# The first block's attention pair by pair of heads, in a written order, with products of zeros between

## Chip, core and metric

The kernel runs on one core of a Trainium2 chip. The metric is the device time of one execution in microseconds (us). The engines are TensorE (PE in the profile, PEld its weight loads), VectorE (DVE), ScalarE (ACT), GpSimd (POOL), and SyncE (SP), which here only issues the loads and stores.

## What is computed

Three layers over 2304 tokens (4 batches of 576) of width 512. The first is linear attention with a norm by head, the second a dense expert layer with a squared ReLU, the third a layer of eight routed experts:

```python
kv  = einsum('bhsd,bhse->bhde', k, v)          # 8 heads of 64
out = einsum('bhsd,bhde->bhse', q, kv)
out = out / sqrt(mean(out * out, -1) + 1e-6) * g_norm
x   = out.transpose(0, 2, 1, 3).reshape(2304, 512)
x   = relu(x @ w_in) ** 2 @ w_out              # 512 -> 2048 -> 512
# then: logits = x @ w_gate, one expert of 8 for each token, up to `capacity` tokens each,
# relu(x @ w1[e]) @ w2[e], times the gate's probability, back to the token's row
```

All inputs are 32-bit floats. The products of the dense layer are made of three passes of a rounded high part and a low part (`PASSES`: high·high, high·low, low·high), and so every operand of theirs has to be split into two tiles first.

## The kernel before

**Blocks and units.** Tokens are worked in six blocks of 384 (three tiles of 128). A unit (j, f) is block j with chunk f of the hidden width (16 chunks of 128): `mm1` makes 12 products of 128x384 into a PSUM bank `pk[s % 2]`, ACT and DVE square and split the result (L282 to L286), and two units later `mm2` adds 9 products of 128x512 into the block's three output banks. Units of block 0 come first, then blocks 0 and 1 by turns, then the others.

**Attention of a block.** `kv(b, p)` multiplies K and V of batch b and pair p of heads (5 products of fp32) and puts the two 64x64 blocks into the block-diagonal matrix `kvb` (ACT L212, DVE L213). `attn_out(t)` multiplies tile t of q with the four pairs into one bank, squares it on ACT (L236), sums by head on DVE (L238), and POOL makes the factor r as a power (L240, L242). `attn_mul` multiplies by r on DVE (L246), `attn_tr` transposes on PE (L255) and writes the high part (ACT, L259) and the low part (DVE, L260) of the operand `xT`. In block 0 this is done tile by tile, so the first output needs all four pairs.

**Weights of the dense layer.** A chunk f has an in-weight and an out-weight, each loaded as 64-bit words (`load_m`). `cvt_m` turns them into fp32: a first pass of ACT (L168, `ch`), then on DVE a first pass (L169) and a second pass (L170) over both weights, and a last pass for each (L174, `cf`). `split_m` rounds to the high part on ACT (L183) and makes the low part on POOL (L184).

**What sets the order.** SP's queue is in the order of the code: K and V of the four pairs of batch 0, then three tiles of q, then chunks 0 and 1 and what follows. The other engines' instructions are put in order by a scheduler's planner; each engine then runs its own list strictly in that order. At the start PE multiplies zeros nine times (`HOT`, L539). The line numbers in the profile are those of this file.

Of the kernel before, what the change touches and what calls it, by code (L numbers as in the profile page):

```python
# [7 lines left out]
F32 = mybir.dt.float32  # L8
F32R = mybir.dt.float32r
BF16 = mybir.dt.bfloat16  # L10
I32 = mybir.dt.int32
# [15 lines left out]
def attn_moe_kernel(ctx: ExitStack, tc: tile.TileContext, cap, kp, vp, qt, gn, wm, wg, wgt, w1, w2, ident, tri, out):  # L27
# [84 lines left out]
    def after_scatters(dma):  # L112
        dma = getattr(dma, "ins", dma)
        for i in scattered["disp"]:
            tc.add_manual_dep(
                dma, i.name, mybir.DependencyInfo(mybir.DependencyClass.Sync, mybir.DependencyReason.DATA),
                reason="reads what the scatters wrote",
            )


    kt, vt, qtt = {}, {}, {}
# [29 lines left out]
    def cvt_m(f):  # L151


        ws = [stg.pop(("m", f, i)).bitcast(I32).rearrange("p (n t) -> p n t", t=2) for i in range(2)]
        if f < 12:
            h = wpool2.tile([P, 2, 512], F32, tag="w", name="ch")
            o = wpool2.tile([P, 2, 512], F32, tag="w", name="cf")
            parts = [(h, o, slice(0, 2))]
            cvt[f] = [o[:, i, :] for i in range(2)]
        else:  # L160
            hs = [(apool1, apool)[i].tile([P, 1, 512], F32, tag="qx"[i], name="ch") for i in range(2)]
            os = [(apool, apool1)[i].tile([P, 1, 512], F32, tag="kv"[i], name="cf") for i in range(2)]
            parts = [(hs[i], os[i], slice(i, i + 1)) for i in range(2)]
            cvt[f] = [o[:, 0, :] for o in os]
        for h, o, sl in parts:
            hi, oi = h.bitcast(I32), o.bitcast(I32)
            for n, w in enumerate(ws[sl]):
                nc.scalar.activation(out=h[:, n, :], in_=w[:, :, 1].bitcast(F32), func=AF.Copy, scale=2.0 ** -112)  # L168
            nc.vector.tensor_scalar(oi, hi, -(1 << 31), None, op0=ALU.bitwise_and)  # L169
            nc.vector.scalar_tensor_tensor(  # L170
                out=oi, in0=hi, scalar=3, in1=oi, op0=ALU.logical_shift_left, op1=ALU.bitwise_or
            )
            for n, w in enumerate(ws[sl]):
                nc.vector.scalar_tensor_tensor(  # L174
                    out=oi[:, n, :], in0=w[:, :, 0], scalar=29, in1=oi[:, n, :],
                    op0=ALU.logical_shift_right, op1=ALU.bitwise_or,
                )

    def split_m(f, pool):
        os = cvt.pop(f)  # L180
        for o, d in zip(os, (wi, wo)):
            w = d[f] = pool.tile([P, 2, 512], F32R, tag="w", name="w")
            nc.scalar.copy(w[:, 0, :], o)  # L183
# [22 lines left out]
    def kv(b, p):  # L206
        k, v = kt.pop((b, p)), vt.pop((b, p))
        ps = misc()
        for c in range(NCH):
            nc.tensor.matmul(ps[:, :P], lhsT=k[:, c, :], rhs=v[:, c, :], start=c == 0, stop=c == NCH - 1)  # L210
# [52 lines left out]
        )  # L263


    gt = {}

    def mm1(s):
        j, f = units[s]
        h = pk[s % 2][:, :BT]  # L270
        n = 0
        for c in range(KD):
            for a, m in PASSES:
                nc.tensor.matmul(  # L274
                    h, lhsT=wi[f][:, a, c * P:(c + 1) * P], rhs=xT[j][:, m, c, :],
                    start=n == 0, stop=n == 3 * KD - 1,
                )
                n += 1


        r = gpool.tile([P, BT], F32, tag="rr", name="rr", bufs=2)
# [245 lines left out]
    MIDDLE = 416  # L527
    units = []

    with tc.manual_schedule(engines={mybir.EngineType.SP}):  # L530

        cold = gpool.tile([P, BT], F32, tag="rr", name="cold", bufs=2)[:, :P]
        nc.vector.memset(cold, 0.0)
# [1 line left out]
        for d in kvb:  # L535
            nc.vector.memset(d, 0.0)

        for i in range(HOT):
            nc.tensor.matmul(pk[0][:, :P], lhsT=cold, rhs=cold, start=True, stop=True)  # L539
# [16 lines left out]
        load_kv(1, 0)  # L556
# [5 lines left out]
        nc.sync.dma_start(out=tri_sb, in_=tri)  # L562
        for t in range(TB, 2 * TB):
            load_q(t)
        for p in range(NPAIR):
            kv(0, p)
        for t in range(TB):
            attn_out(t)
        for t in range(TB):
            attn_mul(t)  # L570
            attn_tr(t)
        for f in range(2):
            cvt_m(f)
            split_m(f, wpool)

        done_b = [1]

# [99 lines left out]
        for s in range(len(units)):  # L677
            j, f = units[s]
            if s == at[1, 0] + LAG:
                free.clear()  # L680
            mm1(s)
            if j == 0 and f + 3 < NF:
                load_m(f + 3)
            if j == 0 and f + 2 < NF:
                cvt_m(f + 2)
                split_m(f + 2, wpool if f + 2 < 12 else wpool2)
            if s >= LAG:
                mm2(s - LAG)
                jj, ff = units[s - LAG]
                if ff == NF - 1:  # L690
                    y_out(jj)
                    if jj < 2:
                        free[:] = ysets[jj]
            for p_ in plan.pop(s, []):
                p_()
            fl = s - at[NB - 1, 0]
# [379 lines left out]
```

## Time and profile before

| | us |
|---|---|
| median of 3 runs | 757.43 |
| lowest and highest | 756.63, 759.12 |
| the profiled execution | 755.1 |
| its span, first to last instruction | 753.2 |
| PE busy in the span | 715.7 |
| DVE busy | 371.6 |
| ACT busy | 309.5 |
| POOL busy | 292.3 |

A share of busy time is a mean over stages with different limits. The stage of this change is the first tenth of the span, where PE has waits; later it is full nearly all the time. In the rows "idle" in brackets is the time that the engine waited before the group, and the arrow names what ended it. An fp32 product of 128x128 leaves two records, and so five products of a pair stand as x10.

### The profile page before, as it was taken

Reading aid. Unit: us, or ns where it says so; the run is one execution under the profiler, and the core shown is the slowest. Engines: PE = TensorE matmul, PEld = TensorE weight load, DVE = VectorE, ACT = ScalarE, POOL = GpSimd, SP = SyncE. Lnnn points to the kernel's source line nnn. Section 1 sums busy time; section 2 is a strip of 40 time slices with the busy share of each in tenths; the row PEclk is TensorE's granted clock in tenths of the full one; section 3 lists DMA queues with packets and bytes.
Section 4 is the critical chain, followed back from the end, with each engine's and each line's share of the span. In section 5 each row is a group of like instructions: output and inputs, shape, how many; then the busy total and the mean of one; then the engine's idle time right before and its main releaser. Section 6 shows DMA issues by size and latency. Waiting matters only on the chain. (4 is left out here: it accounts for less than half of the span.)

```text
span 753.2 us, 12061 instructions
## 1 busy us (share of the span) xinstructions
PE 715.7 (95%) x4012; PEld 637.5 (85%) x4012; DVE 371.6 (49%) x833; ACT 309.5 (41%) x650; POOL 292.3 (39%) x288
## 2 busy tenths in 40 slices
PE   6678999999999999999999999999999999999985
PEld 6667999898899989989898988897888898889764
DVE  2989866548982594349634973331043221133011
ACT  2455454323222332233233264244276544376362
POOL 2566333112022200220130089043469746386881
PEclk9899999999999999999999999999999999999999
DMA  9946798401032202210010176043537554456530
GB/s 326 378 169 201 264 364 293 150 15 67 1 112 87 67 1 70 88 29 0 15 57 1 49 241 204 26 150 121 171 102 219 199 170 148 149 188 212 180 129 19
DMA packets 38016, 102.36 MB, mean 136 GB/s; under 512 B 4451, under 2 KB 4707, under 8 KB 37920
## 3 DMA queue, kind: packets, MB, share of 16 engines
q1 hardware_dynamic: 34912, 91.99, 36.4%
q0 software_dynamic: 3008, 9.10, 3.2%
q8 instruction: 59, 0.97, 0.5%
q14 instruction: 37, 0.30, 0.1%
HBM read 77.78 MB, written 23.91 MB: 135 GB/s over the span
## 5 line engine op out<-in xcount | busy, mean ns | idle before, releaser
L274 PE MATMUL pk<-xT,w 128*128 128x384 f32 x1152 | 223.1, 341 | 8.5 <-POOL w L184 4.6
L293 PE MATMUL pk<-w,g 128*128 128x512 f32 x864 | 218.4, 394 | 2.5 <-ACT g L285 2.5
L274 PEld LDWEIGHTS pk<-xT,w 128*128 128x128 f32 x1152 | 201.5, 188 | 18.6 <-POOL w L184 5.8
L195 POOL TENSOR_TENSOR w<-st,w 128x512 fp32r<-128x512 f32 x128 | 161.5, 1295 | 83.1 <-ACT w L191 83.0
L293 PEld LDWEIGHTS pk<-w,g 128*128 128x128 f32 x864 | 160.2, 188 | 31.7 <-ACT g L285 3.1
L282 ACT ACTIVATE rr<-pk 128x384 f32<-128x384 f32 x96 | 47.1, 492 | 153.6 <-PE pk L274 153.4
L817 PE MATMUL hb<-x,w 128*128 128x256 f32 (+2 forms) x672 | 96.7, 303 | 0.3
L817 PEld LDWEIGHTS hb<-x,w 128*128 128x128 f32 x672 | 93.8, 189 | 1.1 <-issue 0.2
L284 DVE TENSOR_TENSOR pk<-pk,rr 128x384 f32<-128x384 f32 x96 | 54.0, 563 | 74.6 <-ACT rr L282 73.7
L871 DVE SCALAR_TENSOR_TENSOR g<-hb,g 128x576 fp32r<-128x576 f32 (+3 forms) x72 | 40.5, 585 | 97.5 <-ACT g L870 96.5
L103 POOL DMA_INDIRECT disp<-y,sli x18 | 19.1, 1059 | 173.0 <-DVE sli L410 52.9
L355 DVE SCALAR_TENSOR_TENSOR junk<-y,wgb 128x512 f32<-128x512 f32 x120 | 78.0, 684 | 0.7 <-ACT y L313 0.6
L191 ACT CAST w<-st 128x512 fp32r<-128x512 f32 x128 | 71.7, 620 | 13.8 <-DMA st<-in_w 13.4
L285 ACT CAST g<-pk 128x384 fp32r<-128x384 f32 x96 | 46.0, 480 | 72.6 <-DVE pk L284 71.0
L286 DVE TENSOR_TENSOR g<-pk,g 128x384 fp32r<-128x384 f32 x96 | 53.3, 556 | 36.7 <-ACT g L285 36.0
L184 POOL TENSOR_TENSOR w<-cf,w 128x512 fp32r<-128x512 f32 x32 | 47.3, 1494 | 60.9 <-ACT w L183 56.3
L903 PE MATMUL hb<-w,g 128*128 128x512 f32 x264 | 65.7, 407 | 3.1 <-DVE g L871 2.5
L903 PEld LDWEIGHTS hb<-w,g 128*128 128x128 f32 x264 | 50.0, 193 | 15.7 <-DVE g L871 3.4
L870 ACT ACTIVATE g<-hb 128x576 fp32r (+3 forms) x72 | 34.9, 513 | 33.9 <-PE hb L817 29.2
L103 POOL DMA_INDIRECT out<-o,meta x22 | 21.3, 970 | 42.0 <-ACT o L911 17.8
L919 DVE SCALAR_TENSOR_TENSOR o<-bk,meta,o 64x512 f32<-64x512 f32 x3 | 2.3, 752 | 69.5 <-ACT o L918 51.0
L240 POOL TENSOR_SCALAR ms<-ss 128x8 f32<-128x8 f32 x18 | 4.6, 254 | 77.6 <-DVE ss L238 77.3
(138 smaller groups left out, 648.8 us busy)
## 6 DMA issues: line engine op xcount, KB each, us to landing
st<-in_w SPq DMA_DIRECT2D x64, 512.0 KB
st<-in_wm SPq DMA_DIRECT2D x32, 512.0 KB
disp<-zrow SPq DMA_DIRECT2D x9, 1028.0 KB
xr<-disp SPq DMA_DIRECT2D x32, 257.0 KB
k<-in_kp SPq DMA_DIRECT2D x16, 320.0 KB
v<-in_vp SPq DMA_DIRECT2D x16, 320.0 KB
q<-in_qt SPq DMA_DIRECT2D x18, 256.0 KB
out<-zrow SPq DMA_DIRECT2D x9, 512.0 KB
```

Source lines behind the costliest of these rows:

```text
L184: nc.gpsimd.tensor_tensor(w[:, 1, :], o, f32(w[:, 0, :]), op=ALU.subtract)
L191: nc.scalar.copy(w[:, 0, :], s[:, i, :])
L195: e.tensor_tensor(w[:, 1, :], s[:, i, :], f32(w[:, 0, :]), op=ALU.subtract)
L274: nc.tensor.matmul(h, lhsT=wi[f][:, a, c * P:(c + 1) * P], rhs=xT[j][:, m, c, :], start=n == 0, stop=n == 3 * KD - 1,)
L282: nc.scalar.activation(out=r, in_=h, func=AF.Relu)
L284: nc.vector.tensor_tensor(h, h, r, op=ALU.mult)
L285: nc.scalar.copy(g[:, 0, :], h)
L286: nc.vector.tensor_tensor(g[:, 1, :], h, f32(g[:, 0, :]), op=ALU.subtract)
L293: nc.tensor.matmul(ysets[j == 1][i], lhsT=g[:, a, i * P:(i + 1) * P], rhs=wo[f][:, m, :], start=f == 0 and n == 0, stop=f == NF - 1 and n ...
L355: nc.vector.scalar_tensor_tensor(out=junk, in0=yt[j * TB + i][:, :DM], scalar=1.0, in1=wgb[e // 2][:, e % 2, :], op0=ALU.mult, op1=ALU.mul ...
L817: nc.tensor.matmul(h, lhsT=w1_at(e, f // 2, a, c)[:, f % 2 * P:(f % 2 + 1) * P], rhs=x[:, m, c, o:o + w], start=k == 0, stop=k == 3 * KD - 1,)
L903: nc.tensor.matmul(ps[:k, :], lhsT=lhs(f, a), rhs=we2[e, f][:, b, :], start=n == 0, stop=n == len(passes) * NF2 - 1,)
```

## The change

Block 0's attention is written anew, pair by pair. The three tiles of q are loaded right after pair 0. For each pair p, `first_out` makes the three tiles' outputs of this pair (3 products into one bank) and squares them, `first_red` sums and makes the factor, `first_mul` multiplies, `first_tr` transposes and writes the high part, `first_low` the low part; operations on DVE and ACT are 384 wide instead of 512, four times instead of three. The transposes of a pair stand behind the outputs of the next. The pairs use six banks in turn instead of three.

The whole first part is taken out of the planner's hands: all engines run it in the order of the code. Three groups of products of zeros (`warm`, 4, 3 and 6) stand between. Chunk 0 is converted and split in two halves, the in-weight first, behind the low part of pair 2 and before the multiplication of pair 3. From there on the planner works as before, with two bounds on it that are no waits (`in_order`): the conversions of chunk 1 come after the last high part of the attention, those of the next chunk after chunk 1's last rounding, and the products of batch 1's pairs after the first unit's.

```diff
+    def in_order(later, first):
+        tc.add_manual_dep(
+            later, first.name, mybir.DependencyInfo(mybir.DependencyClass.NoSync, mybir.DependencyReason.SCHED_ONLY),
...
-            parts = [(h, o, slice(0, 2))]
+            parts = [(h[:, a:a + n], o[:, a:a + n], slice(a, a + n)) for a, n in (((0, 1), (1, 1)) if f == 0 else ((0, 2),))]
...
+            a = nc.scalar.activation(out=h[:, n, :], in_=w[:, :, 1].bitcast(F32), func=AF.Copy, scale=2.0 ** -112)
+            if "cvt" in marks:
+                in_order(a, marks["cvt"])
...
+    def split_m(f, pool, which=(0, 1)):
+        for i in which:
+            o = cvt[f][i]
...
+            a = nc.tensor.matmul(ps[:, :P], lhsT=k[:, c, :], rhs=v[:, c, :], start=c == 0, stop=c == NCH - 1)
+            if "kv" in marks:
+                in_order(a, marks["kv"])
...
+    def first_out(p):
+        ps = ops[p] = misc()
+        for t in range(TB):
+            nc.tensor.matmul(
+                ps[:, t * P:(t + 1) * P], lhsT=qtt[t][:, p, :], rhs=kvb[0][:, p, :],
+                start=t == 0, stop=t == TB - 1, skip_group_check=True,
+            )
...
+        nc.scalar.activation(out=x, in_=ps[:, :BT], func=AF.Square)
+
+    def first_red(p):
...
+        nc.vector.tensor_reduce(out=ss, in_=x.rearrange("p (h e) -> p h e", e=DH), axis=AX.X, op=ALU.add)
...
+        nc.gpsimd.tensor_tensor(r, ms, expo[:, :2 * TB], op=ALU.pow)
...
+    def first_tr(p):
+        x = xst.pop(p)
+        ps = misc()
+        for t in range(TB):
+            nc.tensor.transpose(ps[:, t * P:(t + 1) * P], x[:, t * P:(t + 1) * P], id_sb)
+        d = xt_tile(0)
+        marks["first"] = nc.scalar.activation(out=d[:, 0, p, :], in_=ps[:, :BT], func=AF.Copy, scale=gn_sb)
...
-    with tc.manual_schedule(engines={mybir.EngineType.SP}):
+    with tc.manual_schedule():
...
-        for p in range(NPAIR):
-            load_kv(0, p)
-            if p == 0:
-                nc.sync.dma_start(out=id_sb, in_=ident)
-                nc.sync.dma_start(out=gn_sb, in_=gn)
+        load_kv(0, 0)
+        nc.sync.dma_start(out=id_sb, in_=ident)
+        nc.sync.dma_start(out=gn_sb, in_=gn)
         for t in range(TB):
             load_q(t)
+        load_kv(0, 1)
+        load_kv(0, 2)
+        load_kv(0, 3)
...
+        free[:] = pk[2:8]
+        kv(0, 0)
+        first_out(0)
+        first_red(0)
+        warm(4)
+        kv(0, 1)
+        first_mul(0)
+        first_out(1)
+        first_red(1)
+        first_tr(0)
+        kv(0, 2)
+        first_low(0)
+        first_out(2)
+        first_mul(1)
+        first_red(2)
+        kv(0, 3)
+        first_out(3)
+        first_red(3)
+        first_tr(1)
+        first_low(1)
+        warm(3)
+        first_mul(2)
+        first_tr(2)
+        first_low(2)
+        c_in, c_out = cvt_m(0)
+        c_in()
+        split_m(0, wpool, (0,))
+        warm(6)
+        first_mul(3)
+        first_tr(3)
+        first_low(3)
+        c_out()
+        split_m(0, wpool, (1,))
...
+    with tc.manual_schedule(engines={mybir.EngineType.SP}):
+        marks["cvt"] = marks["first"]
+        for c in cvt_m(1):
+            c()
+        split_m(1, wpool)
+        marks["cvt"] = marks["split"]
```

PE's list from the pairs of batch 0 to the second unit, before (`v,k` are a pair's products, `kvb,q` the outputs, `id_sb,x` the transposes, `xT,w` the units of the dense layer, and `pk_88`, `pk_89` their banks):

```order
L210 MATMUL pk_93<-v,k 128x128 x5
L228 MATMUL pk_94<-kvb_128,q 128x128 x4
L228 MATMUL pk_95<-kvb_128,q 128x128 x4
L228 MATMUL pk_93<-kvb_128,q 128x128 x4
L255 MATMUL pk_94<-id_sb,x 128x128 x4
L255 MATMUL pk_95<-id_sb,x 128x128 x4
L255 MATMUL pk_93<-id_sb,x 128x128 x4
L210 MATMUL pk_94<-v,k 128x128 x5
L210 MATMUL pk_95<-v,k 128x128 x5
L210 MATMUL pk_93<-v,k 128x128 x5
L210 MATMUL pk_94<-v,k 128x128 x3
L274 MATMUL pk_88<-xT,w 128x384 x2
```

All pairs come first there, then all outputs, then all transposes. The end of the same stretch now (`cold` are the zeros):

```order
L224 MATMUL pk_91<-v,k 128x128 x5
L286 MATMUL pk_92<-kvb_128,q 128x128 x3
L314 MATMUL pk_93<-id_sb,x 128x128 x3
L602 MATMUL pk_88<-cold 128x128 x3
L314 MATMUL pk_94<-id_sb,x 128x128 x3
L602 MATMUL pk_88<-cold 128x128 x6
L314 MATMUL pk_95<-id_sb,x 128x128 x3
L334 MATMUL pk_88<-xT,w 128x384 x12
L224 MATMUL pk_93<-v,k 128x128 x5
L224 MATMUL pk_94<-v,k 128x128 x5
L224 MATMUL pk_95<-v,k 128x128 x5
L334 MATMUL pk_89<-xT,w 128x384 x12
```

The products of batch 1's pairs, which stood ahead of the first unit, now stand behind it.

DVE's list at the end of the attention, before (`st_176` and `st_178` are chunk 0's two weights, `st_180` and `st_182` chunk 1's; `kvb_129` is batch 1's matrix):

```order
L246 TENSOR_TENSOR x<-pk_95,r 128x512
L169 TENSOR_SCALAR cf<-ch 128x1024
L260 SCALAR_TENSOR_TENSOR xT<-pk_94,gn_sb,xT 128x4x128
L260 SCALAR_TENSOR_TENSOR xT<-pk_95,gn_sb,xT 128x4x128
L246 TENSOR_TENSOR x<-pk_93,r 128x512
L170 SCALAR_TENSOR_TENSOR cf<-ch,cf 128x1024
L169 TENSOR_SCALAR cf<-ch 128x1024
L260 SCALAR_TENSOR_TENSOR xT<-pk_93,gn_sb,xT 128x4x128
L174 SCALAR_TENSOR_TENSOR cf<-st_176,cf 128x512
L174 SCALAR_TENSOR_TENSOR cf<-st_178,cf 128x512
L170 SCALAR_TENSOR_TENSOR cf<-ch,cf 128x1024
```

The conversions stand between the attention's steps there. DVE's list at the same place now:

```order
L321 SCALAR_TENSOR_TENSOR xT<-pk_94,gn_sb,xT 128x384
L183 TENSOR_SCALAR cf<-ch 128x512
L184 SCALAR_TENSOR_TENSOR cf<-ch,cf 128x512
L188 SCALAR_TENSOR_TENSOR cf<-st_176,cf 128x512
L305 TENSOR_TENSOR x<-pk_92,r 128x384
L321 SCALAR_TENSOR_TENSOR xT<-pk_95,gn_sb,xT 128x384
L183 TENSOR_SCALAR cf<-ch 128x512
L184 SCALAR_TENSOR_TENSOR cf<-ch,cf 128x512
L183 TENSOR_SCALAR cf<-ch 128x1024
L188 SCALAR_TENSOR_TENSOR cf<-st_178,cf 128x512
L184 SCALAR_TENSOR_TENSOR cf<-ch,cf 128x1024
```

The first passes of chunks 0 and 1 and chunk 0's second pass, which stood between the attention's steps, now come one weight at a time, chunk 0's in-weight before the last multiplication and everything else after the last low part.

## Rows read from the trace of the kernel before

**Rows 1.** The page, part 1: busy us (share of the span) and instructions, TensorE

```profile
PE 715.7 (95%) x4012; PEld 637.5 (85%) x4012; DVE 371.6 (49%) x833; ACT 309.5 (41%) x650; POOL 292.3 (39%) x288
```

**Rows 2.** Table by stretches: from:to, length, busy of each engine, granted clock, DMA share, GB/s

```profile
5.00:10.00 5.00, 3.19 (x23) 2.86 (x22) 0.77 (x5) 0.41 (x2) 0.00 (x0) 1.00 0.98 330
10.00:15.00 5.00, 4.76 (x40) 4.52 (x41) 0.95 (x3) 1.24 (x4) 0.00 (x0) 1.00 1.05 414
15.00:20.00 5.00, 1.26 (x10) 0.85 (x8) 2.88 (x6) 2.75 (x5) 4.38 (x6) 0.94 1.03 400
20.00:25.00 5.00, 2.63 (x12) 2.29 (x13) 4.27 (x6) 2.20 (x4) 2.14 (x4) 0.50 1.03 402
...
30.00:35.00 5.00, 2.93 (x16) 2.41 (x14) 4.89 (x4) 1.70 (x4) 5.00 (x4) 1.00 1.04 414
...
75.00:80.00 5.00, 5.00 (x27) 4.47 (x26) 4.44 (x7) 2.64 (x6) 2.12 (x2) 1.00 0.94 315
```

**Rows 3.** Timeline of TensorE: start us, busy us, engine, line, operation, tiles, count, [idle before]

```profile
7.70 1.35 PE L210 MATMUL pk<-v,k 128*128 128x128 f32 x10 [1.02 <-DMA v<-in_vp]
...
11.44 1.35 PE L210 MATMUL pk<-v,k 128*128 128x128 f32 x10 [0.24 <-DMA v<-in_vp]
...
18.11 0.63 PE L255 MATMUL pk<-id_sb,x 128*128 128x128 f32 x4 [2.49 <-DVE x L246]
20.12 1.08 PE L255 MATMUL pk<-id_sb,x 128*128 128x128 f32 x4 [1.38 <-DVE x L246]
...
24.34 5.30 PE L210 MATMUL pk<-v,k 128*128 128x128 f32 x36
...
31.16 2.39 PE L274 MATMUL pk<-xT,w 128*128 128x384 f32 x12 [0.63 <-POOL w L184]
35.08 2.03 PE L274 MATMUL pk<-xT,w 128*128 128x384 f32 x10 [1.52 <-POOL w L184]
...
37.16 1.06 PE L228 MATMUL pk<-kvb,q 128*128 128x128 f32 x8
```

**Rows 4.** Table by stretches, the 27.7 us in which DVE is nearly full

```profile
26.10:53.80 27.70, 22.88 (x139) 19.72 (x138) 24.65 (x32) 15.79 (x33) 18.27 (x13) 1.00 0.74 268
```

**Rows 5.** Timeline of all engines: steps of the attention, first roundings and low parts

```profile
9.33 0.23 DVE L213 COPY kvb<-pk 64x64 f32<-64x64 f32 x1 [1.80 <-ACT kvb L212]
...
14.50 0.69 DVE L238 TENSOR_REDUCE ss<-x 128x8 f32<-128x512 f32 x1 [1.21 <-ACT x L236]
...
17.28 0.69 DVE L246 TENSOR_TENSOR x<-pk,r 128x512 f32<-128x512 f32 x1 [1.19 <-POOL r L242]
...
25.30 0.75 DVE L260 SCALAR_TENSOR_TENSOR xT<-pk,gn_sb,xT 128x512 fp32r<-128x512 f32 x1 [0.26 <-ACT xT L259]
...
29.03 2.18 ACT L183 CAST w<-cf 128x512 fp32r<-128x512 f32 x4
...
29.73 9.91 POOL L184 TENSOR_TENSOR w<-cf,w 128x512 fp32r<-128x512 f32 x6 [7.51 <-ACT w L183]
```

**Rows 6.** DVE by line and shape, 0 to 27 us: count, busy us, mean ns, idle

```profile
L169 DVE TENSOR_SCALAR cf<-ch 128x1024 int32<-128x1024 int32 x2 | 1.4, 682 | 0.0
L174 DVE SCALAR_TENSOR_TENSOR cf<-st,cf 128x512 int32<-128x512 int32 x2 | 1.3, 682 | 0.0
L170 DVE SCALAR_TENSOR_TENSOR cf<-ch,cf 128x1024 int32<-128x1024 int32 x1 | 1.2, 1212 | 0.0
```

**Rows 7.** Timeline of DVE: a second pass beside POOL, and the last row considered

```profile
31.70 2.20 DVE L170 SCALAR_TENSOR_TENSOR cf<-ch,cf 128x1024 int32<-128x1024 int32 x1
...
53.83 0.69 DVE L246 TENSOR_TENSOR x<-pk,r 128x512 f32<-128x512 f32 x1 [0.94 <-POOL r L242]
```

**Rows 8.** DVE by line and shape, 26.1 to 53.8 us: the conversions

```profile
L174 DVE SCALAR_TENSOR_TENSOR cf<-st,cf 128x512 int32<-128x512 int32 x10 | 8.9, 933 | 0.1
L170 DVE SCALAR_TENSOR_TENSOR cf<-ch,cf 128x1024 int32<-128x1024 int32 x4 | 6.3, 1584 | 0.0
L169 DVE TENSOR_SCALAR cf<-ch 128x1024 int32<-128x1024 int32 x3 | 2.8, 920 | 0.0
```

More of the change, by code (lines that the diff above doesn't have):

```diff
@@ L118, in after_scatters @@
             )
+    def in_order(later, first):
+        later, first = getattr(later, "ins", later), getattr(first, "ins", first)
+        tc.add_manual_dep(
+            later, first.name, mybir.DependencyInfo(mybir.DependencyClass.NoSync, mybir.DependencyReason.SCHED_ONLY),
+            reason="the order in which the loads come in",
+        )
+    marks = {}
     kt, vt, qtt = {}, {}, {}
@@ L164, in cvt_m, with cvt_part @@
             cvt[f] = [o[:, 0, :] for o in os]
[L165 to L169, printed above, removed]
+        return [lambda part=part: cvt_part(ws, *part) for part in parts]
+    def cvt_part(ws, h, o, sl):
+        hi, oi = h.bitcast(I32), o.bitcast(I32)
+        for n, w in enumerate(ws[sl]):
+            a = nc.scalar.activation(out=h[:, n, :], in_=w[:, :, 1].bitcast(F32), func=AF.Copy, scale=2.0 ** -112)
+            if "cvt" in marks:
+                in_order(a, marks["cvt"])
+        nc.vector.tensor_scalar(oi, hi, -(1 << 31), None, op0=ALU.bitwise_and)
+        nc.vector.scalar_tensor_tensor(
+            out=oi, in0=hi, scalar=3, in1=oi, op0=ALU.logical_shift_left, op1=ALU.bitwise_or
+        )
+        for n, w in enumerate(ws[sl]):
             nc.vector.scalar_tensor_tensor(
-                out=oi, in0=hi, scalar=3, in1=oi, op0=ALU.logical_shift_left, op1=ALU.bitwise_or
-            )
[L173 to L183, printed above, removed]
+                out=oi[:, n, :], in0=w[:, :, 0], scalar=29, in1=oi[:, n, :],
+                op0=ALU.logical_shift_right, op1=ALU.bitwise_or,
+            )
+    def split_m(f, pool, which=(0, 1)):
+        for i in which:
+            o = cvt[f][i]
+            w = (wi, wo)[i][f] = pool.tile([P, 2, 512], F32R, tag="w", name="w")
+            marks["split"] = nc.scalar.copy(w[:, 0, :], o)
             nc.gpsimd.tensor_tensor(w[:, 1, :], o, f32(w[:, 0, :]), op=ALU.subtract)
@@ L263, in attn_tr, with first_mul, first_low @@
         )
+    def first_out(p):
[4 more added lines that the diff above has]
+                start=t == 0, stop=t == TB - 1, skip_group_check=True,
+            )
+        x = xst[p] = ypool.tile([P, ROW], F32, tag="y", name="x")[:, :BT] if p < 3 else apool.tile(
+            [P, DM], F32, tag="x", name="x")[:, :BT]
+        nc.scalar.activation(out=x, in_=ps[:, :BT], func=AF.Square)
+    def first_red(p):
+        x = xst[p]
+        ss = small.tile([P, 2 * TB], F32, tag="ss", name="ss")
+        nc.vector.tensor_reduce(out=ss, in_=x.rearrange("p (h e) -> p h e", e=DH), axis=AX.X, op=ALU.add)
+        ms = small.tile([P, 2 * TB], F32, tag="ms", name="ms")
+        nc.gpsimd.tensor_scalar(ms, ss, 1.0 / DH, 1e-6, op0=ALU.mult, op1=ALU.add)
+        r = rst[p] = small.tile([P, 2 * TB], F32, tag="r", name="r")
+        nc.gpsimd.tensor_tensor(r, ms, expo[:, :2 * TB], op=ALU.pow)
+    def first_mul(p):
+        r, ps = rst.pop(p), ops.pop(p)
+        nc.vector.tensor_tensor(
+            xst[p].rearrange("p (h e) -> p h e", e=DH), ps[:, :BT].rearrange("p (h e) -> p h e", e=DH),
+            r.rearrange("p (h o) -> p h o", o=1).to_broadcast([P, 2 * TB, DH]), op=ALU.mult,
+        )
+    def first_tr(p):
[5 more added lines that the diff above has]
+        marks["first"] = nc.scalar.activation(out=d[:, 0, p, :], in_=ps[:, :BT], func=AF.Copy, scale=gn_sb)
+        ops[p] = ps
+    def first_low(p):
+        d, ps = xt_tile(0), ops.pop(p)
+        nc.vector.scalar_tensor_tensor(
+            out=d[:, 1, p, :], in0=ps[:, :BT], scalar=gn_sb, in1=f32(d[:, 0, p, :]), op0=ALU.mult, op1=ALU.subtract,
+        )
     gt = {}
@@ L536, in attn_moe_kernel, with warm @@
             nc.vector.memset(d, 0.0)
-        for i in range(HOT):
-            nc.tensor.matmul(pk[0][:, :P], lhsT=cold, rhs=cold, start=True, stop=True)
+        def warm(n):
+            for _ in range(n):
+                nc.tensor.matmul(pk[0][:, :P], lhsT=cold, rhs=cold, start=True, stop=True)
+        warm(HOT)
         nc.gpsimd.iota(tok, pattern=[[P, NT]], base=0, channel_multiplier=1)
@@ L564, in attn_moe_kernel @@
             load_q(t)
-        for p in range(NPAIR):
-            kv(0, p)
-        for t in range(TB):
[L568 to L574, printed above, removed]
+        free[:] = pk[2:8]
[31 more added lines that the diff above has]
+        split_m(0, wpool, (1,))
+        for t in range(TB):
+            qtt.pop(t)
+        free[:] = ysets[1]
+    with tc.manual_schedule(engines={mybir.EngineType.SP}):
[4 more added lines that the diff above has]
+        marks["cvt"] = marks["split"]
         done_b = [1]
@@ L684, in attn_moe_kernel @@
             if j == 0 and f + 2 < NF:
-                cvt_m(f + 2)
+                for c in cvt_m(f + 2):
+                    c()
+                marks.pop("cvt", None)
                 split_m(f + 2, wpool if f + 2 < 12 else wpool2)
```

7 lines of the change are left out of this document (5 added, 2 removed).

## Prediction

> **What bounds the kernel now.** I read the page's busy times first: TensorE (PE) is busy 95% of the span [rows 1], so a change in the first stage is worth only the PE time that it takes out of the start. The table by stretches comes next: PE is full from 75 us on [rows 2], and until then it has holes. The timeline of PE shows what they are: waits for loads up to 11.4 us, then for the transposes' input, then for weights: the first expert product runs at 31.16, the second chunk's at 35.08, and everything up to the first tile of block 1 is done at 37.16 + 1.06 = 38.2 us [rows 3]. The last look is at VectorE (DVE) between 26.1 and 53.8 us. It is busy 24.65 of 27.70 us there [rows 4], and what PE waits for at that time (weights, hidden values, tiles of block 1) has gone through it. So two things bound the start: first the serial chain of the attention, then DVE's queue. A gain in the first counts only as far as DVE's queue also ends sooner.
>
> **The loads.** SP's queue now asks for the three q tiles right behind pair 0 and before pairs 1 to 3. The bytes in front of the weights are the same, so no weight lands earlier or later. Before, pair 1 came in by 7.70 and pair 3 by 11.44 us [rows 3]. 0.79 MB of q now stand where 0.66 MB of pair 1 stood: at the rates of [rows 2] (330 GB/s in 5 to 10 us, 414 in 10 to 15) q is there at about 8.05, pair 1 at 10.2, pair 2 at 11.8 and pair 3 at 13.3 us.
>
> **The chain of the attention.** Five fp32 products, two records each, take 1.35 us [rows 3], so three take 0.8. From the end of a pair's products to its block on the diagonal I take 0.5 us (ACT copy, then the DVE copy of 0.23), from the start of the reduction to the multiplication 17.28 - 14.50 = 2.78, at three quarters of the width 2.6, and for a DVE step of 0.69 to 0.75 us some 0.55 [rows 5]; ScalarE's steps alike. Walked: pair 0's outputs start with q, 8.1 to 8.9 (before, no output could start until pair 3's products had ended at 11.44 + 1.35 = 12.8 [rows 3]); square and the 2.6 us put its multiplication at 12.0 and its end at 12.6. Pair 1's products run 10.2 to 11.55, its outputs, 0.5 later, to 12.9, and behind them on PE the transposes of pair 0 to 13.4; pair 2 to 14.75, outputs 15.25 to 16.1; pair 3 to 17.45, outputs 17.95 to 18.8; transposes of pair 1 at 19.3. Pair 2's square, 2.6 us and multiplication lead from 16.1 to 21.1, so its transposes end at 21.7. Then DVE, whose order is now written out, converts the first half of chunk 0 (0.35 + 0.62 + 0.62, half of [rows 6]) before it multiplies pair 3: that ends at 25.2, its transposes at 25.8, its low part at 26.9. Before, the last low part ended at 25.30 + 0.75 = 26.05 [rows 5]. So the attention of the first block, though it starts 4 us earlier, ends 0.85 us later: 17 us of single file with DVE waiting in each step.
>
> **The zeros and the clock.** 13 products of zeros at 0.27 us stand where PE waits anyway: 8.9 to 9.95 (pair 1 comes at 10.2), 19.3 to 20.1 (next needed 21.2), 21.7 to 23.3 (25.2). They cost nothing; if pair 1 landed sooner, at most 0.3. What they may keep is the clock: before, PE did 1.26 us of work in 15 to 20 us, then the granted clock fell to 0.50 [rows 2] and four transposes took 1.08 instead of 0.63 us [rows 3]. In the walk above PE works 2.3 us of 20 to 25, between that 1.26 and the 2.93 that held at 30 to 35 [rows 2]. If it falls, ten of the first expert products (0.2 us each [rows 3]) double, up to 2.0 us, but ScalarE takes them up only at 30.2 (it rounds the second half of chunk 0 first), so the sum has 0 for it and 0.4 as the far end. POOL's two short tasks for later buffers stand between the factors of pairs 2 and 3, and one waits for the transposes of pair 1; pair 3's factors are there at 22, needed at 24.7, so this is hidden, with 2.7 us to spare.
>
> **The first expert products.** Chunk 0's first weight is rounded at 24.7 and its low part made by 26.7, against 29.03 [rows 5] and 31.1, for which the row of 31.16 waited [rows 3]: the first unit ends at 28.9 instead of 33.2 (ten more products from 31.16 on [rows 3]). That is 4.3 us. But products of batch 1's pairs, which filled PE's waits before (36 half passes in 5.30 us [rows 3]), now stand behind it: three pairs, 4.05 us, to 33.0. The second unit needs chunk 1, whose conversion DVE now begins at 28.3 (before, its first pass and chunk 0's were both done by 27 us [rows 6]): its low part comes at about 34.1, and it ends at 36.2 against 37.1. The fourth pair (1.35) and the first tile of block 1 (1.06) then end at 38.6, against 38.2. The 4.3 us are used up: the same work is done at the same time, in another order.
>
> **DVE's queue.** From 26.1 us to the multiplication at 53.83 [rows 7], DVE spent 27.70 us: 3.05 idle, and 24.65 busy [rows 4]. Of the busy time, the conversions lost (933-682) ns x 10 + (1584-1212) x 4 + (920-682) x 3 = 4.7 us against their prices before 27 us [rows 6, 8]: POOL's low parts run beside them here, not there. So 19.95 us are work. In the changed order the same multiplication has more ahead of it, from 26.9 on: the first and second pass of half of chunk 0 (0.34 + 0.62) and chunk 1's first pass (0.60), but one last pass less (0.60), so about 1.0 us more. 26.9 + 19.95 + 1.0 = 47.85, plus what is lost. With the same 7.75 us lost it is 55.6, 1.8 us behind. I estimate less: chunk 0's first low part (25.3) meets only operations that read PSUM; the others meet part of chunk 1's second pass (0.4), chunk 2's first (0.6), chunk 3's first and second (1.7), chunk 4's (1.2): 3.9 to 4.0. Idle: 1.1 where DVE waits at about 33.9 for ScalarE's first pass of chunk 2 (its queue has two roundings and two copies first), 0.5 for a tile's factors (0.94 in the last row [rows 7]), and some 0.6 of short gaps: 2.2. So 47.85 + 4.0 + 2.2 = 54.05, +0.2 us. From there on both programs have the same instructions in the same order, so this difference stays to the end. Bounds: losses of 3 to 9.5 us, -3 to +3.5.
>
> A rule to weigh here: the row of 31.70 shows a second pass at 2.20 us beside POOL where 1.21 is its price alone [rows 6, 7], so I let both run on at half pace. [...]
>
> **The rivals.** *The gain carries.* POOL's low parts all fall beside PSUM reads, so 1.5 us of stretch and 1.3 of waits remain: 47.85 + 2.8 = 50.65, 3.2 us ahead, 754.2. For it: the lows start 4.4 us earlier and come two at a time, not six in a row [rows 5]. Against: every chunk still has two lows and 3.2 us of passes, and DVE has no slack to step aside. *DVE stays behind.* The place is 27 to 45 us: DVE enters 0.85 us late with 1.0 us more to do; if the lost time is not smaller than before (7.75) and ScalarE's late first pass of chunk 2 (1.1) comes on top, +2.9 us: 760.3. It counts as slower from losses of 8.3 us on (2.3 us behind). For it: the written order lets nothing overtake in the first 27 us. Against: the run of six lows on end is gone. *The clock falls early.* If the pauses of 12 to 26 us already take it, 5.5 us of products on the chain double and everything follows: 762.9. The zeros and 3.9 us of work in 15 to 20 speak against it. That the change would not do what it says can be left out: the order shows it.
>
> **How the numbers follow.** The profiled execution took 755.1 us (span 753.2, 1.9 around it); the median of the runs is 757.43, 2.3 more. The sum, +0.2, makes 755.3 for such an execution and 757.6 for the median. Chances: forecast 0.76, the gain carries 0.12, DVE stays behind 0.10, the clock 0.02. A measurement of this kernel can tell about 0.3%, 2.3 us, from no change, so faster 0.12, same 0.76, slower 0.12. The range takes in no change on both sides, and half of the slower rival: 755.0 to 760.2; most of the first rival and the last are left out.
>
> **What would show it.** Right: first unit's products end near 29 us, the low part of pair 3 ends near 27, the second unit ends within 1 us of 37, PE is full from 75 to 76 us, and DVE's conversions between 27 and 54 us lose 3 to 5 us. Wrong: PE full by 73 us (DVE lost under 3.7 us in all), or only from 78 on; a granted clock of 0.50 before 22 us; a low part of pair 3 later than 28.5.

## The result: slower by 4.6 us, and where it shows

| | before | after |
|---|---|---|
| median of 16 runs each | 756.72 us | 761.76 us |
| lowest and highest | 755.03, 759.96 | 758.18, 766.66 |
| the profiled execution (its span) | 755.1 (753.2) | 758.18 (756.4) |

The ratio is 1.0061, with a 95% interval of 1.0046 to 1.0077; in a second set of runs (7 of after) it is 1.0070 (1.0044 to 1.0097). The forecast was no change, 757.6 us, with 755.0 to 760.2 as its range: it is wrong, and by a mechanism that none of its cases held.

The page, part 1, after, for [rows 1]; 26 more records of PE are the 13 products of zeros, two for each:

```profile
PE 718.8 (95%) x4038; PEld 640.2 (85%) x4038; DVE 370.4 (49%) x838; ACT 310.2 (41%) x652; POOL 291.1 (38%) x290
```

The table by stretches of after, for [rows 2] and [rows 4] (columns as there):

```profile
5.00:10.00 5.00, 4.15 (x26) 3.56 (x24) 0.41 (x2) 0.70 (x2) 0.00 (x0) 1.00 0.99 354
...
15.00:20.00 5.00, 3.98 (x31) 3.60 (x31) 2.75 (x7) 1.66 (x4) 3.44 (x6) 1.00 1.02 391
20.00:25.00 5.00, 1.89 (x15) 1.70 (x15) 3.67 (x7) 1.35 (x3) 1.52 (x2) 1.00 1.03 407
...
26.84:30.25 3.41, 3.41 (x11) 3.41 (x12) 3.37 (x6) 2.00 (x4) 0.00 (x0) 0.50 1.04 356
...
27.20:53.40 26.20, 22.86 (x140) 20.34 (x140) 23.75 (x35) 16.23 (x34) 15.30 (x12) 0.94 0.75 266
```

The timeline of PE in after, for [rows 3]: first outputs, first and second unit, first tile of block 1, and the last wait before PE is full:

```profile
7.59 1.67 PE L286 MATMUL pk<-kvb,q 128*128 128x128 f32 x6 [0.62 <-DVE kvb L229]
...
26.83 3.56 PE L334 MATMUL pk<-xT,w 128*128 128x384 f32 x10 [0.58 <-POOL w L198]
...
34.43 2.03 PE L334 MATMUL pk<-xT,w 128*128 128x384 f32 x10 [0.34 <-POOL w L198]
...
37.41 1.06 PE L244 MATMUL pk<-kvb,q 128*128 128x128 f32 x8
...
70.85 2.63 PE L355 MATMUL pk<-w,g 128*128 128x512 f32 x6 [2.48 <-ACT g L347]
73.28 2.87 PE L334 MATMUL pk<-xT,w 128*128 128x384 f32 x12
...
76.69 2.28 PE L334 MATMUL pk<-xT,w 128*128 128x384 f32 x12
```

DVE in after, for [rows 5, 7]: the low part of pair 3, and the multiplication to which the prediction's sum was made:

```profile
26.55 0.62 DVE L321 SCALAR_TENSOR_TENSOR xT<-pk,gn_sb,xT 128x384 fp32r<-128x384 f32 x1 [1.31 <-ACT xT L316]
...
53.35 0.67 DVE L262 TENSOR_TENSOR x<-pk,r 128x512 f32<-128x512 f32 x1
```

So the first stage went as walked: the low part of pair 3 ends at 27.2 us (forecast 26.9), the second unit at 36.5 (36.2), the first tile of block 1 at 38.5 (38.6), and the multiplication is at 53.35 (54.05), half a microsecond ahead of before instead of 0.2 behind. PE is then full from 76.69 us on, against 75.58 in the profiled execution of before; but that is the granted clock, which fell to 0.50 behind the wait at 70.85 here and not in that execution. In another execution of before it fell there too, and PE is full from 77.17 on:

```profile
71.58 2.93 PE L293 MATMUL pk<-w,g 128*128 128x512 f32 x6 [2.45 <-ACT g L285]
...
77.17 2.28 PE L274 MATMUL pk<-xT,w 128*128 128x384 f32 x12
```

Like for like the start is 0.5 us ahead. The loss lies behind 500 us, in the routed experts, which the diff does not touch. Their code has branches: by an expert's count of tokens each engine jumps over the products that it doesn't need. Four places in TensorE's list are used below: **A**, the transposes behind the first expert's branches, near 517 us; and in the last expert **B**, two transposes near 725, **C**, its first products `hb<-w,x` near 735, and **D**, its third group `bk<-w,x` near 740. The timeline of PE there, before:

```profile
517.34 1.08 PE L796 MATMUL bk<-id_sb,xr 128*128 128x128 f32 x8 [1.34 <-issue]
...
723.21 0.30 PE L859 MATMUL hb<-id_sb,turned 128*128 128x128 f32 x1 [0.29 <-issue]
...
725.73 7.34 PE L903 MATMUL hb<-w,g 128*128 128x512 f32 x24 [0.99 <-DVE g L871]
...
733.25 1.66 PE L842 MATMUL hb<-w,x 128*128 128x256 f32 x12
...
738.05 1.69 PE L842 MATMUL bk<-w,x 128*128 128x256 f32 x12
```

And after, the same instructions in the same order:

```profile
519.84 1.08 PE L899 MATMUL bk<-id_sb,xr 128*128 128x128 f32 x8 [2.48 <-issue]
...
726.86 0.41 PE L962 MATMUL hb<-id_sb,turned 128*128 128x128 f32 x2 [1.35 <-ACT gl L979]
...
734.71 1.68 PE L945 MATMUL hb<-w,x 128*128 128x256 f32 x12 [0.51 <-issue]
...
741.20 1.67 PE L945 MATMUL bk<-w,x 128*128 128x256 f32 x12 [1.51 <-ACT gl L979]
```

A waits 1.1 us longer, B 1.1, C 0.5, D 1.5. "issue" says that nothing in the profile released A and C. `gl`, named at B and D, is only the last thing that ACT had done; what these need is a copy `turned` (the operand of B's transposes, and the bank that D writes), and the timeline of ACT in after has both copies done 1.2 and 1.3 us before B and D start:

```profile
725.32 0.37 ACT L964 COPY turned<-bk 128x256 f32<-128x256 f32 x1 [0.66 <-PE bk L945]
...
739.50 0.37 ACT L964 COPY turned<-bk 128x256 f32<-128x256 f32 x1 [0.22 <-PE bk L945]
```

Over the whole stretch from full speed to the last product, PE's idle time in the records is 13.2 us before and 16.7 after. With 1.1 us at the start, and 1.5 that before lost in 726.0 to 729.4 us at half clock (24 products in 7.34 us, 5.82 at full clock) and after did not, that is 1.1 + 3.5 - 1.5 = 3.1 of the 3.2 us between the two spans.

### The profile page after: what moved, and what is told of

It reads as the page before. It is cut to its first block, busy times and chain, and to the rows that moved or that the text cites. A ratio compares the mean times of both kernels' runs of the same rounds, so it can differ in the third digit from the quotient of the medians.

```text
span 756.4 us, 12119 instructions
## 1 busy us (share of the span) xinstructions
PE 718.8 (95%) x4038; PEld 640.2 (85%) x4038; DVE 370.4 (49%) x838; ACT 310.2 (41%) x652; POOL 291.1 (38%) x290
## 5 line engine op out<-in xcount | busy, mean ns | idle before, releaser
L334 PE MATMUL pk<-xT,w 128*128 128x384 f32 x1152 | 225.9, 343 | 6.3 <-POOL w L198 3.3
L346 DVE TENSOR_TENSOR pk<-pk,rr 128x384 f32<-128x384 f32 x96 | 54.0, 563 | 75.4 <-ACT rr L344 74.5
L205 ACT CAST w<-st 128x512 fp32r<-128x512 f32 x128 | 71.6, 620 | 13.4 <-DMA st<-in_w 12.9
L198 POOL TENSOR_TENSOR w<-cf,w 128x512 fp32r<-128x512 f32 x32 | 44.6, 1409 | 64.2 <-ACT w L197 59.6
L1006 PE MATMUL hb<-w,g 128*128 128x512 f32 x264 | 64.1, 399 | 2.1 <-DVE g L974 1.8
L973 ACT ACTIVATE g<-hb 128x576 fp32r (+3 forms) x72 | 34.9, 512 | 33.9 <-PE hb L920 26.1
```

The costliest lines, as they stand in the source:

```text
L205: nc.scalar.copy(w[:, 0, :], s[:, i, :])
L334: a = nc.tensor.matmul(h, lhsT=wi[f][:, a, c * P:(c + 1) * P], rhs=xT[j][:, m, c, :], start=n == 0, stop=n == 3 * KD - 1,)
L1006: nc.tensor.matmul(ps[:k, :], lhsT=lhs(f, a), rhs=we2[e, f][:, b, :], start=n == 0, stop=n == len(passes) * NF2 - 1,)
```

## Experiments

Three theories stood against each other: the clock (zeros at the start, a lower clock later), the written order of the first stage, and, once the waits at A to D had been seen, the place of TensorE's code: how many of its instructions stand ahead. One 32-bit product is four of them (two weight loads, two products, as the records show), so the 13 zeros are 52; the changed kernel's code stands 51 further back, since it has one wait fewer (407 records of waits and branches on TensorE, 408 before).

**Both kernels again, the zeros away, more zeros.** The zeros: `warm` 4, 3, 6 to none; and 3 to 8, 6 to 15.

```diff
-        warm(4)
...
-        warm(3)
+        warm(8)
...
-        warm(6)
+        warm(15)
```

> The kernel before once more, for a second trace and the granted clock of each of its executions. Clock theory (the 4.6 us are TensorE's clock, granted low in more stretches of the changed kernel): mean granted clock about 0.991 in most executions, and times that rise where it is lower. Queue theory (the written order makes a later start of the full stretch at full clock): no difference of clock between the kernels; this one 757 us with TensorE full from 75.6 us.

> The changed kernel once more. Clock theory: 761 to 763 us, mean granted clock 0.985 to 0.989, and in the trace at least two more stretches at 0.5 than in the first trace, which had two ahead of the tail (26.8 and 71.2 us) and was the quickest of its 16 executions. Queue theory: the same stretches at 0.5 as in the first trace, and TensorE full only 3 to 4 us later than before's 75.6 us with the clock full.

> The changed kernel without its 13 products of zeros behind the start (output unchanged; the nine at the very start stay). Clock theory: the clock falls earlier or for longer before 30 us, and the time is 1 to 3 us longer than the changed kernel's. Queue theory, and my prediction's sum: they stand in waits, so no change (within 1 us).

> The changed kernel with 8 and 15 products of zeros instead of 3 and 6 ahead of the transposes of pairs 2 and 3, which fills the waits of 1.28 and 2.37 us there. Clock theory: the first units run at full clock (the first one's last ten products 2.0 instead of 3.6 us), mean granted clock up by 0.004 or more, 1.5 to 4 us less than the changed kernel. Queue theory: first unit 1.5 us sooner, but the end no more than 0.5 us sooner, since DVE's queue is not.

Measured: before again 756.4 us (ratio 0.9999, 0.998 to 1.0019), after again 760.21, no zeros 759.74 (1.0040, 1.0024 to 1.0056), more zeros 763.34 (1.0097, 1.0067 to 1.0128). The clock theory falls: over all executions the mean granted clock is 0.988 before and 0.988 after, and without zeros it is 0.981, yet that kernel is no slower than after. At an equal clock the loss stands: the executions with a mean of 0.990 or more took 754.5 us on average before (22 of them) and 758.9 after (6). Without zeros the clock fell early, and PE came to full speed at 82.3 us, 5.1 us later than in the execution of before that had a fall at 71 us too (the traced execution without zeros is the slowest of nine):

```profile
11.30:21.60 10.30, 8.63 (x38) 7.84 (x37) 3.43 (x8) 2.18 (x6) 4.19 (x7) 0.50 1.03 409
```

So the zeros do what they are for: in these traces they save some 5 us of start. But the kernel without them is no slower for it: behind full speed it waits 14.1 us, after 16.7, more zeros 18.4. The waits grow with zeros that ran 450 us earlier. That is where the third theory comes from.

**The code moved, nothing more executed.** 26 short products (52 instructions) on a side of a branch that is not taken, just ahead of A:

```diff
                 with done.Else():
+                    for _ in range(26):
+                        nothing(bk[0], P)
                     tr_x(0, 0)
```

> The kernel before with 26 short products (52 TensorE instructions) added on a side of a branch that is not taken, ahead of the routed experts from 517 us on: nothing more is executed, but every later TensorE instruction stands 52 places further back, as in the changed kernel (whose 13 products of zeros are 52 instructions). Theory of the place of the code: TensorE's waits behind branches from 517 us on are waits for its own instructions and depend on where the jumps' targets stand; so they become those of the changed kernel: 2.5 us instead of 1.0 to 1.3 ahead of the transposes at 517 to 520, 1.2 to 1.4 and 1.2 to 1.5 us at two places after 720 us that had none; in all 3.5 to 4 us more from 517 us on, median 759.5 to 760.5. Theory of the clock: the zeros keep the clock high early and have it low later; without executed zeros nothing changes, 756 +- 0.7. Theory of the written order: 756 +- 0.7 too.

757.17 us (1.0022, 1.0002 to 1.0042): 1.7 us slower for code that never ran. B waits 1.22 us and D 0.84, where before had 0.29 and none; A stays at 0.94. A's wait is not set by what is skipped directly ahead of it, and the forecast of all of the loss was too much.

**Fewer, wider zeros.** The changed kernel with the same columns of zeros in 9 products instead of 22:

```diff
-        warm(HOT)
+        warm(BT, BT, P)
...
-        warm(4)
+        warm(BT, P)
...
-        warm(3)
+        warm(BT)
...
-        warm(6)
+        warm(BT, BT, 8)
```

> The changed kernel with the same columns of zeros in 9 products instead of 22 (384 wide instead of 128): the zeros run as long, but TensorE's code is 52 instructions shorter ahead of everything else and stands where that of the kernel before stands. Theory of the place of the code: the waits from 517 us on go back to those of before (1.0 to 1.3 us, and none at the two places after 720 us), 3.5 to 4 us less than the changed kernel: 756.5 to 758. Theory of the clock: the zeros are there, so it stays at 760.2 to 761.8. Theory of the written order: 760.2 to 761.8 too.

757.93 us (1.0027, 1.0004 to 1.0050): more than half of the loss is gone, as the place theory said, with A at 1.45, B at 0.29 and nothing at D. C waits 2.09 us, which was not expected, and all waits behind full speed add up to 16.5 us in this trace, as in after. The traced execution, 759.58, is the second slowest of its twelve; the two of after, 758.18 and 758.04, are the fastest of theirs.

**Code moved behind A.** The same branch with 54 and with 78 short products in the changed kernel.

> The changed kernel with 54 short products (108 TensorE instructions) on the side of the branch that is not taken. Nothing more is executed. Theory of the place of the code: the waits behind branches from 517 us on change in size and place, by up to 4 us in sum either way; no forecast of the sign. Clock and written order: 760.2 to 761.8 with the same waits as the changed kernel.

> The changed kernel with 78 short products (156 TensorE instructions) on the side of the branch that is not taken; nothing more is executed. Theory of the place of the code: as with 108, other waits again; where the place is 207 behind that of before, it is nearer to a whole block of 256 instructions behind it (the trace fetches TensorE's instructions in pieces of 16 KB), so the waits should be nearer to those of before, 757 to 760. Clock and written order: 760.2 to 761.8.

761.68 (1.0077, 1.0051 to 1.0103) and 762.75 us (1.0099, 1.0062 to 1.0137). A is 2.51 and 2.44, as in the changed kernel, though 108 and 156 more instructions are skipped there. B, C and D wait 1.55, none and 0.77 us in the first, 1.10, 1.34 and none in the second. That the second would come nearer to before was a miss.

**The deciding pair: 52 instructions more in the kernel before.** Its 9 zeros of 128 columns as 7 of 128 and 15 of 8, all at the start:

```diff
-        for i in range(HOT):
-            nc.tensor.matmul(pk[0][:, :P], lhsT=cold, rhs=cold, start=True, stop=True)
+        for w in (P,) * 7 + (8,) * 15:
+            nc.tensor.matmul(pk[0][:, :w], lhsT=cold, rhs=cold[:, :w], start=True, stop=True)
```

> The kernel before with 22 products of zeros at its start instead of 9, 7 of them 128 wide and 15 only 8 wide: they take about as long as the 9, but TensorE's whole code stands 52 instructions further back, as in the changed kernel. Theory of the place of the code: the waits behind branches become those of the changed kernel: 2.4 to 2.5 us ahead of the transposes at 517 (1.0 to 1.3 before), 1.2 to 1.4 us ahead of the two transposes near 723 (0.3 before) and 1.2 to 1.5 us ahead of the products near 738 (none before); 3.2 to 3.8 us more, median 758.0 to 759.5. Theory of the first stage (what makes the changed kernel slower is done in its first 80 us): 755.5 +- 0.7 and the waits of before.

760.57 us (1.0058, 1.0036 to 1.0080): the whole loss of the change, without the change. Its timeline of PE has the waits of after at A, B and D:

```profile
518.73 1.08 PE L796 MATMUL bk<-id_sb,xr 128*128 128x128 f32 x8 [2.53 <-issue]
520.04 7.38 PE L903 MATMUL hb<-w,g 128*128 128x512 f32 x24 [0.23 <-ACT x L801]
...
726.90 0.41 PE L859 MATMUL hb<-id_sb,turned 128*128 128x128 f32 x2 [1.41 <-ACT gl L876]
...
742.54 1.67 PE L842 MATMUL bk<-w,x 128*128 128x256 f32 x12 [1.73 <-ACT gl L876]
```

Here the granted clock also fell, to 0.50, in the products behind A: 24 took 7.38 us, where those of before took 5.86 at full clock. Over all executions its mean clock is 0.986, that of before in the same set 0.988; 0.002 of 756 us is some 1.5 us, so a part of the loss may be clock (worked out, not shown). The other zeros at the start cost nothing in the trace: the last wait ahead of full speed ends at 71.66 us here, at 71.28 and 71.58 in the traces of before.

**Small moves.** The kernel before with one zero in 16 bits (2 instructions fewer: in the traces the product and the weight load of a 16-bit product leave one record each); the changed kernel with fewer zeros and 2 or 10 instructions more:

```diff
-        warm(BT, BT, 8)
+        warm(BT, BT)
+        half = cold.bitcast(mybir.dt.bfloat16)
+        for _ in range(3):
+            nc.tensor.matmul(pk[0][:, :8], lhsT=half[:, :P], rhs=half[:, :8], start=True, stop=True)
```

> The kernel before with one of the 9 products of zeros in 16 bits and 8 wide, 2 instructions for 4: TensorE's code stands 2 instructions further forward. Theory of the place of the code: the two kernels whose code stood 1 further forward (the changed one without zeros, and with fewer and wider zeros) had a wait of 1.2 to 2.1 us ahead of the product that follows the block at 735 to 741 us, the kernel before has none; if the place decides sharply, it is here too, 1 to 2 us more: 756.5 to 757.5. If not, 755.5 +- 0.7, and that wait came from the executed zeros or the order.

> The changed kernel with fewer, wider zeros, and three zeros in 16 bits (6 instructions) for its last short product of 4: TensorE's code stands 1 instruction behind that of the kernel before, instead of 1 ahead of it. Theory of the place of the code: the wait of 2.1 us at 734 to 736 us goes, the others stay: 1 to 2 us less than the kernel with fewer zeros, 755.5 to 757. Theory of the first stage: 757.9 +- 0.8 as that kernel.

> The same with seven zeros in 16 bits: TensorE's code stands 9 instructions behind that of the kernel before. Theory of the place of the code: no wait at 734 to 736 us either; the wait at 517 us between 1.0 and 2.5: 755.5 to 757.5. Theory of the first stage: 757.9 +- 0.8.

755.66 (0.9986, 0.9964 to 1.0007), 757.37 (1.0006, 0.9984 to 1.0027) and 758.63 us (1.0030, 1.0005 to 1.0054). C's wait is in all three (1.68, 1.59, 1.78), so a sharp edge at the place of before is refuted. What differs in both traces of before, and in three others that have no wait at C, is the clock: the products ahead of C ran at 0.50, in before for 3.4 us (the row of 725.73, 7.34 us), and afterwards PE did not have to wait. With them at full clock (5.82 us) it waits at C instead, and starts C as late. In this place a low clock cost nothing. It does not always replace the wait: with 156 instructions skipped at A the 24 products took 8.34 us, and C waits 1.34 all the same.

**A whole piece further.** The page shows code being loaded in packets of 16 KB: 59 on this queue before, 60 after. They go with TensorE's instructions: from the start of the packet at 77.60 us to that at 461.19, 16 packets later, the trace of before has 4106 of them (2043 weight loads, 2043 products, 20 waits), 256.6 a packet; after, from 71.99 to 480.99 us, 17 packets and 4355, 256.2.

```profile
q8 instruction: 60, 0.98, 0.5%
```

The changed kernel with its 22 zeros as 147 in 16 bits (45, 25, 35, 42; 48 wide) has 206 instructions more, and stands 257 behind before. By the 256 to 257 instructions a packet that is one piece, to within an instruction or so (an estimate from the two traces).

> The changed kernel with its 22 products of zeros in 32 bits (88 TensorE instructions) as 147 in 16 bits and 48 wide (294 instructions), in the same four places: TensorE's code stands 257 instructions behind that of the kernel before, one whole piece of 16 KB (256 instructions) and 1. Theory that the place within such pieces decides: the waits are those of the kernels whose code stands at -1 to +9: 1.0 to 1.5 us ahead of the transposes near 519 us (2.5 in the changed kernel), 0.3 ahead of the two transposes near 726 (1.2 to 1.4), none near 741 (1.2 to 1.5), 1.2 to 2.1 near 735; from full speed on as the kernel with fewer zeros and one instruction more, 757.4, plus what the start loses by the other zeros (0 to 2 us). Theory that more instructions cost more (13 zeros 4.6 us, 27 zeros 7.4 us, so every instruction of TensorE's start some 0.07 us later): at least the waits of the changed kernel and more, 765 or above.

759.31 us (1.0040, 1.0022 to 1.0059), with the waits of the kernel at +1, not those of a kernel with ever more instructions (A, B, C; none at D):

```profile
521.28 1.08 PE L900 MATMUL bk<-id_sb,xr 128*128 128x128 f32 x8 [1.04 <-issue]
...
728.18 0.30 PE L963 MATMUL hb<-id_sb,turned 128*128 128x128 f32 x1 [0.29 <-issue]
...
738.38 1.66 PE L946 MATMUL hb<-w,x 128*128 128x256 f32 x12 [1.79 <-ACTq L1038]
```

Its 1.9 us over the kernel at +1 fit the start: in the two traces PE is full 2.3 us later. Its ratio alone would not tell it from after (1.0046 to 1.0077); its waits speak for the place within a piece, and against the number of instructions.

**Forward.** The kernel before with its 9 zeros as 3 of 384 columns, in search of a place that beats both.

> The kernel before with its 9 products of zeros of 128 columns as 3 of 384: the same columns, 24 TensorE instructions fewer, so the code stands 24 places further forward. Theory of the place of the code: the waits from 517 us on are others than at 0 (13.2 to 13.4 us in sum from full speed on, 14.5 at -2); if the waits grow on both sides of the place of the kernel before, 14 to 16 us, median 756 to 758; if they shrink forward, 11 to 13 us and 753 to 755, which would be faster than both kernels.

758.63 us (1.0040, 1.0021 to 1.0059), slower: C waits 2.42 and the group ahead of B 2.04 us. No version beat the kernel before by more than the noise.

All places together (TensorE instructions ahead, against before; waits in us from the profiled execution of each; "-" under 0.2; where a kernel was profiled twice, both):

| place | kernel | ratio to before | A | B | C | D |
|---|---|---|---|---|---|---|
| -24 | before, 3 wide zeros | 1.0040 | 1.02 | - | 2.42 | - |
| -2 | before, 2 fewer | 0.9986 | 1.01 | 0.29 | 1.68 | - |
| -1 | after, no zeros | 1.0040 | 1.30 | 0.29 | 1.24 | - |
| -1 | after, fewer zeros | 1.0027 | 1.45 | 0.29 | 2.09 | - |
| 0 | before | 1 | 1.34, 0.98 | 0.29, 0.29 | - | - |
| 1 | after, fewer zeros | 1.0006 | 1.31 | 0.29 | 1.59 | - |
| 9 | after, fewer zeros | 1.0030 | 1.28 | 0.29 | 1.78 | - |
| 51 | after | 1.0061, 1.0070 | 2.48, 2.47 | 1.35, 1.19 | 0.51, 0.37 | 1.51, 1.17 |
| 52 | before, 52 more | 1.0058 | 2.53 | 1.41 | - | 1.73 |
| 107 | after, more zeros | 1.0097 | 1.27 + 2.39 | 1.39 | 0.32 | 0.89 |
| 257 | after, 147 zeros | 1.0040 | 1.04 | 0.29 | 1.79 | - |
| 0, and 52 skipped ahead of A | before, moved | 1.0022 | 0.94 | 1.22 | - | 0.84 |
| 51, and 108 skipped ahead of A | after, moved | 1.0077 | 2.51 | 1.55 | - | 0.77 |
| 51, and 156 skipped ahead of A | after, moved | 1.0099 | 2.44 | 1.10 | 1.34 | - |

**What the waits end with.** Each packet of code has its times in the traces. In ten of the sixteen traces one is asked for ahead of A, and A starts 1.53 to 1.63 us after it has landed (in before it landed at 515.81 us, and A starts at 517.34). C starts 1.51 to 1.59 us after one in twelve traces, with those of before among them, where it shows no wait. B and D in after start 1.6 us after one. In the five traces in which A waits 2.4 to 2.5 us, two packets are asked for within 0.4 us in place of one (in after they landed at 517.55 and 517.56 us, and A starts at 519.84, 2.3 us later); with more zeros A waits twice, each time for one. The queue's packets around A, in after (514.5 to 520 us) and in the second execution of before (516 to 520.5):

```profile
q8 instruction: 2, 0.03, 4.0%
...
q8 instruction: 1, 0.02, 1.4%
```

## Why the prediction was wrong

**The loads, the chain of the attention, the first expert products: right.** Each time on the way lies within 1.5 us of the walk, and the gain of the early start was used up as the text said. (Pair 2's steps as the text names them, from 16.1 us on, make 19.8 and not 21.1; its transposes did start at 21.12, since DVE's written order has pair 3's reduction and pair 1's low part ahead of the multiplication.) (PE full "from 75 to 76 us" was missed by 0.7 us, by the low clock behind the wait at 70.85, which executions of before have too.) Without the zeros PE is full 5 us later, so the rival in which the clock falls early was real, and the zeros are what kept it away.

**The zeros and the clock: right in the first stage, with one size off.** The granted clock did fall in the first unit, 26.84 to 30.25 us, and its ten products took 3.56 us. The sum had 0 for it and 0.4 as the far end; the second unit, at 36.5, shows that it was hidden.

**DVE's queue: right, 0.7 us too pessimistic.** Its conversions by line and shape, 26.5 to 53.4 us after, for [rows 8]:

```profile
L184 DVE SCALAR_TENSOR_TENSOR cf<-ch,cf 128x1024 int32<-128x1024 int32 x4 | 6.3, 1587 | 0.1
L188 DVE SCALAR_TENSOR_TENSOR cf<-st,cf 128x512 int32<-128x512 int32 x9 | 6.1, 709 | 0.0
L183 DVE TENSOR_SCALAR cf<-ch 128x1024 int32<-128x1024 int32 x4 | 4.0, 988 | 1.0 <-ACT ch L180 1.0
```

Against the prices of [rows 6] they lose 9 x 0.027 + 4 x 0.375 + 4 x 0.306 = 3.0 us (forecast 3.9 to 4.0, an estimate from the one row of 31.70; before 4.7), and the last passes run nearly at their price alone. Up to 80 us, operations that read PSUM took the same beside a low part (L184 before, L198 after) as without one, as the walk had it: before 0.56 and 0.55 us at L284, 0.74 and 0.74 at L260; after 0.56 and 0.56 at L346, 0.62 and 0.62 at L321. DVE is idle 26.20 - 23.75 = 2.45 us (2.2).

**The step that failed** is the last sentence of the part on DVE's queue, "From there on both programs have the same instructions in the same order, so this difference stays to the end", together with "They cost nothing" of the zeros. The order was the same; the place of the code was not. The zeros were priced by the time that they run, which is hidden, and not by the 52 instructions that they push between the start and every later branch. That term was 0 in the sum, and measures +4.4 us alone (the kernel before with 52 more, 1.0036 to 1.0080). With it the forecast of 757.6 would have been 762.0, or 761.3 on the 756.72 that before took beside the result; 761.76 was measured. With the code at -1 to 9 the changed kernel is at 1.0027, 1.0006 and 1.0030 of before, 0.5 to 2.3 us behind where 0.2 was forecast: inside the range, but two of the three are slower clear of noise, and what that rest is made of is not shown.

What carries the term is shown in part. Against the kernel before, 1.5 to 3.5 us are waits in the traces (16.5 and 16.7 us behind full speed in after, 16.0 in the kernel with 52 more; 13.2 and 13.4 in before, 14.5 in the kernel with 2 fewer, which had no low clock there). But the changed kernel with its code at -1, 1, 9 and 257 waits 16.5, 15.4, 16.0 and 15.8 us in its one trace each, nearly as long as at 51, and its ratios are 0.2 to 0.6% lower. With one or two traced executions of each, where these 2 to 5 us lie stays open. Of the executions of after that were not traced, this can be said: their mean clock is the same as before's, but the traces of before spend 6.8 us at 0.50 between 19 and 27 us, where PE waits anyway, and those of after 3.4 us in that stage; with the same mean, after has some 3.4 us more of it later, where PE is full and loses half. That share, 1.7 us, is worked out, not shown.

That the waits are for code rests on five facts: nothing in the profile releases A; the places are behind branches; moving code that is not executed moves the waits at B and D; at 257, a whole 16 KB piece behind the kernel at +1, they are nearly what they are there; and A and C start at the same distance, 1.5 to 1.6 us, behind a landed piece of code in kernel after kernel. It is the author's conclusion from these; how TensorE's code is fetched around a branch was not shown. The waits at A are 0.94 to 2.53 us in the traces. At place 51 two pieces are fetched ahead of A in place of one, and A waits longer (2.48 and 2.47 us in after, 1.34 and 0.98 in before); why they are two at that place, and why B and D wait there, stays open.

## What to carry to other kernels

An instruction that costs no time where it runs still takes up code, and 52 of them made 1.0058 here: in a program with branches, count what a change adds on each engine ahead of the branches, and look at the waits behind them ("issue", or a releaser that had ended long before) in both traces. To judge a change of the first stage, keep the place of the later code the same (fewer, wider fillers), or run the old kernel with as many empty instructions; otherwise a part of the comparison, 4.4 us here, belongs to the place. And "the same instructions in the same order" did not mean the same time here: with 52 instructions more at the start of the kernel before, TensorE waited 2.53, 1.41 and 1.73 us at A, B and D, against 1.34, 0.29 and none.

## What was not expected of the hardware

- 52 TensorE instructions more at the start of a program cost 4.4 us (1.0058), and the waits that carry a part of it stand 500 us later; 205 more again bring those at A, B and D back to what they were.
- Behind a branch TensorE went on 1.5 to 1.6 us after the piece of code had landed (A in ten traces, C in twelve).
- Code on a side of a branch that is never taken cost 1.7 us (1.0022, 1.0002 to 1.0042).
- The low clock at 726 us cost nothing: the 1.5 us that the products lost there were waited for at C, 1.6 to 1.8 us, in traces at full clock, and C started 1.6 us behind its piece of code either way.
- The zeros of 4, 3 and 6 products save 5 us of the start: in the trace without them the clock is at 0.50 from 11.3 to 21.6 and from 25.0 to 35.2 us.
